# The ramp of a spectral-filter and SiLU kernel on Trainium2: first stage by parts of the position index, eight PSUM banks, second products issued two groups ahead, weight roundings moved

## The chip, the core and the metric

The kernel runs on one core of one Trainium2 chip. The metric is the device time of one execution in microseconds (us); the time of a version is the median of several runs. Engines are named as the profile names them: PE (TensorE, with PEld for its weight loads), DVE (VectorE), ACT (ScalarE), POOL (GpSimd) and SP (SyncE, which here only issues DMAs). ACT and POOL issue DMAs too.

## The reference, cut to what matters

```python
# x [8, 3008, 256]; filt_r, filt_i [1505, 256]
X = np.fft.rfft(x, axis=1)
Y = X * (filt_r + 1j * filt_i)[None]
y = np.fft.irfft(Y, n=3008, axis=1)          # [8, 3008, 256]
# bridge: 24064 tokens of 256 channels; w_in [256, 2048], w_out [2048, 256]
h = y.reshape(24064, 256) @ w_in
g = h * (1.0 / (1.0 + np.exp(-h)))
out = g @ w_out
```

The MLP's weights arrive as 64-bit floats. The kernel reads them as words and rounds them to 32 bits itself.

## The kernel before, in words

**Main stage.** Each batch's 3008 tokens are cut in six pairs of token blocks (`PAIRS` by two halves), 48 pairs in all, and each pair takes 8 steps, one for each 256 columns of the hidden layer: 384 steps. In a step `hidden` computes the products with w_in into the PSUM tiles px (tag "x") and pyz (tag "yz"), with sums and SiLU on DVE and ACT, and `project` multiplies the step before with w_out into four accumulators (tags a0 to a3). Each step also carries pieces of the next batch's transform, put at written-out places by `plan`.

**Ramp.** Before step 0 the transform of batch 0 has to be done at least for half of its tokens, and the first weights have to be rounded. This part is written out in its own order, lines 865 to 931, and the schedule is manual: every engine executes its instructions in the order in which the code issues them, and waits at each for what that one needs. The pieces are:

- `load_first` (L275) loads batch 0 into two tiles: positions n' 0 to 23 of each row into the space of w_t, positions 24 to 31 into x_all.
- `stage1_first(k)` (L289), k = 0 to 15, 16 channels each: two matmuls (L293) into one PSUM bank, 384 columns from the first tile and 128 columns from the second, and a 32x32 block transpose on DVE (L295) into t2.
- `forward(g)`, g = 0 to 5: 32 matmuls (L428) into two banks pb. It needs all 16 transposes.
- `multiply(g, k)`: two DVE products (L443) of a bank with the two filter tables, into the tiles z (four buffers) and p (two buffers in each of two pools). With two k this makes four products a group, each 128x512.
- `add(g, k)`: two POOL instructions (L451, L452) that combine z and p. For the groups in `by_tensor` there is no add, and PE does the sum with twice the matmuls.
- `inverse_first(g, added)`: 32 matmuls (L485), or 64 for the groups in `by_tensor`, into two banks pc; then two ACT copies into q (L490), each stored by an ACT-issued DMA (L492) into the DRAM array d2. A group makes 8 of the 48 rows of d2. The 64-matmul form reads the tables `neg`, which lie in the two buffers of tag "t".
- `load_t4(g, first, last)`: loads rows of d2 in another layout, in two DMAs (h = 0, 1; L517). Groups 2 and 3 use the buffers of tag "t" in the ramp, so these loads wait until PE is done with `neg`.
- `stage3(g)`, g = 0 to 3: 64 PE records (L529) into two banks pd, each copied to y by `evac`, which alternates between DVE (L244) and ACT (L246).
- `weights(j)` loads the words of weight block j (two DMAs of 256 KB, L781 and L784, on SP). `rounded(j...)` rounds a pair of blocks (L801 to L818, DVE and ACT by turns), places them in w_t (L827), and, after the odd block, makes four combinations (L611) in `combine_weights`.
- `bank` (L251) hands out PSUM banks for batch 0 by turns from six: two of tag "f" and a0 to a3.

22 dummy matmuls (tile "idle", tag "x") run on PE at the start. In the order before, the groups follow each other: forward, multiply, add (not in groups 1, 4, 5), the roundings of blocks 2 and 3 behind group 1's products and of blocks 4 and 5 behind group 4's, and `inverse_first(g - 1)` one group later. The first rows of t4 (0 to 39) are loaded ahead of `rounded(6, 7)` and the last inverse, rows 40 to 47 behind it, half of those on POOL's queue. Then `rounded(8)`, and stage 3. The first matmul px of step 0 needs all eight y copies.

DMAs issued from SP and ACT report on eight semaphores by turns. A DMA waits for the last one on its own semaphore to land before it is issued, and the engine that issues it waits with it.

Of the kernel before, what the change touches and what calls it, by code (L numbers as in the profile page):

```python
# [46 lines left out]
FP32 = mybir.dt.float32  # L47
# [6 lines left out]
B, S, C = 8, 3008, 256  # L54
DFF = 2048
N1, N2 = 47, 64
NS, NG = 24, 6
# [110 lines left out]
def kernel(  # L168
# [9 lines left out]
    nc = tc.nc  # L178
# [10 lines left out]
    def pool(name, bufs, space=None):  # L189
        kw = {} if space is None else {"space": space}  # L190
        return ctx.enter_context(tc.tile_pool(name=name, bufs=bufs, **kw))
# [17 lines left out]
    xps = pool("xps", 1, PSUM)  # L209
# [3 lines left out]
    wx_t = cpool.tile([96, 128], FP32)  # L213
# [9 lines left out]
    x_all = xpool.tile([128, 2, 2, 2 * C], FP32)  # L223
# [14 lines left out]
    flip, early = [0], [0]  # L238

    def evac(dst, src):  # L240

        flip[0] ^= 1
        if flip[0]:
            nc.vector.tensor_copy(out=dst, in_=src)  # L244
        else:
            nc.scalar.copy(out=dst, in_=src)  # L246
# [3 lines left out]
    def bank(b, name, spare=None):  # L250


        if b > 0 and spare is not None:
            return accps.tile([128, 2, C], FP32, name=name, tag=f"a{spare}")
        if b > 0 or early[0] is None:
            return fps.tile([128, 2, C], FP32, name=name, tag="f")
        early[0] += 1
        k = early[0] % 6
        if k < 2:
            return fps.tile([128, 2, C], FP32, name=name, tag="f")  # L260
        return accps.tile([128, 2, C], FP32, name=name, tag=f"a{k - 2}")

    def spectral(b):
# [4 lines left out]
        xs, us, t2s, banks, prods, halves, t4s = {}, {}, {}, {}, {}, {}, {}  # L268
# [17 lines left out]
            us["t2"] = view[:, 6144:14336].rearrange("p (s c) -> p s c", c=C)  # L286
            return view

        def stage1_first(k):  # L289

            ps = bank(b, f"pa_{b}_{k}").rearrange("p a c -> p (a c)").rearrange("p (n c) -> p n c", c=16)
            for i, n0, n in ((0, 0, 24), (1, 24, 8)):
                nc.tensor.matmul(out=ps[:, n0:n0 + n], lhsT=wx_t, rhs=xs[i][0:96, :, 16 * k:16 * k + 16],  # L293
                                 start=True, stop=True)
            nc.vector.transpose(out=us["t2"][:, :, 16 * k:16 * k + 16].rearrange("p s c -> p c s"),  # L295
                                in_=ps.rearrange("p n c -> p c n"))

        def load_x(u):

# [20 lines left out]
        def stage1(u):  # L320
            t1 = tpool.tile([128, 2, 2, C], FP32, name=f"t1_{b}_{u}", tag="t")
            ps = [bank(b, f"pa_{b}_{u}_{h}") for h in range(2)]
            if b == 1:
                xt = xs.pop(u)
# [185 lines left out]
        def load_t4(g, first=0, last=2 * NS):  # L510
            if first == 0 and b == 0 and g in (2, 3):
                t4s[g] = tpool.tile([128, 4, C], FP32, name=f"t4_{b}_{g}", tag="t")
            elif first == 0:
                t4s[g] = t4pool.tile([128, 4, C], FP32, name=f"t4_{b}_{g}", tag="t4")
            for h in range(2):
                queue = nc.gpsimd if first > 0 and h == 1 else nc.sync
                queue.dma_start(out=t4s[g][64 * h + first:64 * h + last],  # L517
                                in_=d2[first:last, 4 * g:4 * g + 4, h, :])

        def stage3(g):  # L520
            half, n0 = divmod(4 * g, 16)
            ps = [bank(b, f"pd_{b}_{g}_{h}").rearrange("p a c -> p (a c)")[:, 0:8 * N1]
                  .rearrange("p (a i n) -> p a i n", a=2, i=4) for h in range(2)]
            for cb in range(2):
                for i in range(4):
                    for c0 in (0, 64):
                        for h in range(2):
                            rows = slice(64 * h, 64 * h + 2 * NS)
                            nc.tensor.matmul(  # L529
                                out=ps[h][c0:c0 + 64, cb, i, :],  # L530
                                lhsT=t4s[g][rows, i, 128 * cb + c0:128 * cb + c0 + 64],
                                rhs=wi_t[rows, :], start=True, stop=True)
            if g < 6 and (b > 0 or g > 3):
                load_t4(g + 2)
            if n0 == 0:
                y[b, half] = ypool.tile([128, 2, HALF], FP32, name=f"y_{b}_{half}", tag="y")
            dst = y[b, half].rearrange("p a (r h n) -> p a h n r", h=2, n=16)
            for h in range(2):
                evac(dst[:, :, h, n0:n0 + 4], ps[h])

        return dict(load_first=load_first, stage1_first=stage1_first, load_x=load_x, sums=sums, stage1=stage1, reverse_x=reverse_x,
                    load_fold=load_fold, fold=fold, stage1_fold=stage1_fold, evict_fold=evict_fold,
# [64 lines left out]
    v, gp = nc.vector, nc.gpsimd  # L607
    ty, g_t, acc, unfinished = {}, {}, {}, []

    def combine(eng, out, in0, in1, op):  # L610
        eng.tensor_tensor(out=out, in0=in0, in1=in1, op=op)  # L611
# [149 lines left out]
    def load_weights(j):  # L761

        if j in (8, 13):
            raw = upool.tile([128, 2, 512], U32, name=f"raw_{j}", tag="u")
        else:

            if j in (0, 2):
                raws["at"] = ypool.tile([128, 2, HALF], FP32, name=f"raw_{j}", tag="y").rearrange(
                    "p a n -> p (a n)").bitcast(U32)[:, 0:2048]
                raws["y"] = raws["at"]  # L770
            elif j in (4, 11):
                raws["at"] = raws["s"] = spool.tile([128, 2048], U32, name=f"raw_{j}", tag="s")
# [12 lines left out]
        raws[j] = raw  # L785
# [55 lines left out]
    def combine_weights(jp, part=None):  # L841

        def w(c):
            return w_t[:, jp, c]
        if part != 1:
            combine(v, w(S1), w(S3), w(A22), ALU.add)
            combine(v, w(S2), w(S1), w(A11), ALU.subtract)
        if part != 0:
            combine(v, w(S3), w(A11), w(S3), ALU.subtract)
            combine(v, w(S4), w(A12), w(S2), ALU.subtract)  # L850

    def weights(*js):
        for j in js:
            if wide:
                load_weights(j)

    def rounded(*js, part=None):

        if wide and part != 1:
            round_weights(*js)  # L860
        for j in js:
            if wide and part != 0:
                place_weights(j)
            if not wide and part != 0:
                load_exact(j)
# [7 lines left out]
        for i in range(2):  # L873
            nc.gpsimd.memset(bias_t[32 * j:32 * j + 32, 3 + i:4 + i], 1.0 if j % 2 == i else -1.0)

    ps = xps.tile([128, 512], FP32, name="idle", tag="x")
    for _ in range(22):
        nc.tensor.matmul(out=ps[:, 0:128], lhsT=wx_t, rhs=wx_t, start=True, stop=True)
    part, second = spectral(0), spectral(1)
    weights(0, 1)  # L880
    place = part["load_first"]()
# [16 lines left out]
    for i, scale in enumerate((-1.0, bias_t[:, 4:5])):  # L898
        t = tpool.tile([128, 4, C], FP32, name=f"neg_{i}", tag="t").rearrange("p a c -> p (a c)")
        neg.append(t[:, 0:128 * NG].rearrange("p (g k n) -> p g k n", g=NG, k=2))  # L900
        nc.scalar.activation(out=neg[i], in_=e_t[:, :, :, 0], func=AFT.Identity, scale=scale)
    for k in range(16):
        part["stage1_first"](k)
    for u in range(2):
        second["load_x"](u)
    rounded(0, 1, part=1)
    by_tensor = (1, 4, 5)
    for g in range(NG):
        part["forward"](g)
        for k in range(2):  # L910
            part["multiply"](g, k)
        if g == 0:
            combine_weights(0)
        if g not in by_tensor:
            for k in range(2):
                part["add"](g, k)
        if g in (1, 4):
            rounded(*((2, 3) if g == 1 else (4, 5)))
            weights(*((9, 10) if g == 1 else (11, 12)))
        if g > 0:  # L920
            part["inverse_first"](g - 1, g - 1 not in by_tensor)
    for g in range(4):
        part["load_t4"](g, 0, 40)
    rounded(6, 7)
    part["inverse_first"](NG - 1, False)
    for g in range(4):
        part["load_t4"](g, 40, 2 * NS)
    rounded(8)
    weights(13)
    for g in range(4):  # L930
        part["stage3"](g)
    early[0] = None
# [79 lines left out]
```

## Time and profile before

| What | Value |
|---|---|
| median of 9 runs | 2616.73 us (2615.58 to 2618.15) |
| the profiled execution, its own time | 2617.84 us |
| its span | 2616.0 us |
| mean granted PE clock | 0.989 |
| PE busy over the span | 2570.1 us (98%) |
| DVE, ACT, POOL busy | 65%, 42%, 16% |
| first matmul px of step 0 starts at | 100.92 us |
| PE busy in the first two slices of 40 | 0.7 and 0.7 (in tenths 7, 7), 0.9 or more from the third on |

Busy time counts the instructions that the profiler recorded on an engine. A PE matmul with 32-bit data leaves two records. "Granted clock" is the TensorE clock as a share of full speed; the profile gives it for any stretch of the span. A view by stages gives, for each stretch, the length, then busy us (and instructions) of PE, PEld, DVE, ACT and POOL, then the granted clock, the share of the DMA engines and their GB/s. In the chain of waits, each line has a start, a length and a piece of work, and each piece was released by the one before it.

### The profile page before, as it was taken

The page shows a single profiled execution, that of the slowest core. Times are in us where ns is not written, and L with a number is a line of the kernel's source. Part 1 is how long each engine was busy: PE and PEld are TensorE (multiplying, and loading weights), DVE is VectorE, ACT ScalarE, POOL GpSimd, SP SyncE. Part 2 cuts the span into 40 slices and gives each one's busy share as a digit, 9 for nine tenths or more (in the row PEclk, how much of TensorE's full clock was granted, in tenths as well). Part 3 has the DMA queues.
Part 4 walks back from the last instruction along what each step waited for, and adds up shares of the span by engine and source line. Part 5 has one row for each costly group of instructions (what it writes and reads, how often), then busy time and mean ns, then how long its engine had stood idle before and what let it go on. Part 6 is the DMA issues. An engine that isn't in the chain of part 4 may idle for free.

```text
span 2616.0 us, 48142 instructions
## 1 busy us (share of the span) xinstructions
PE 2570.1 (98%) x18828; PEld 2184.7 (84%) x18828; DVE 1703.6 (65%) x3588; ACT 1106.9 (42%) x3013; POOL 420.2 (16%) x660
## 2 busy tenths in 40 slices
PE   7799999999999999999999999999999999999998
PEld 4578888888888888888888888888888888888987
DVE  6666766676666666667666676666766666555555
ACT  2443444444444444444444444444444444444443
POOL 1121121112111211121113111211122112101100
PEclk8799999999999999999999999999999999999999
DMA  8431222212322122222222222232223311211000
GB/s 263 126 97 53 62 70 72 70 46 64 82 68 65 51 81 64 57 66 75 68 52 66 73 70 60 68 77 54 66 65 71 78 45 29 57 21 21 9 16 16
DMA packets 200236, 171.06 MB, mean 65 GB/s; under 512 B 122276, under 2 KB 174212, under 8 KB 199220
## 3 DMA queue, kind: packets, MB, share of 16 engines
q1 hardware_dynamic: 178664, 117.20, 18.4%
q0 software_dynamic: 16832, 44.20, 5.4%
q10 hardware_dynamic: 4512, 6.59, 0.8%
q8 instruction: 148, 2.42, 0.4%
q14 instruction: 80, 0.66, 0.1%
HBM read 96.05 MB, written 81.26 MB: 68 GB/s over the span
## 4 chain that ended last, share of the span: by engine, by line
PE 94%; DVE 2%; DMA 2%; ACT 1%; issue 0%; ACTq 0%; SPq 0%; POOL 0%; DVEq 0%; POOLq 0%
PE acc L699 43%; PE px L640 25%; PE pyz L640 19%; PE pd L529 3%; PE pb L428 2%; PE pc L464 2%; PE pf L398 1%; DVE g L611 1%; PE pa L335 0%; DMA w_t<-in_x_dram 0%; PE pc L485 0%; DVE w_t L611 0%; DMA filt<-in_filt_r_dram 0%; DMA d_t<-d_tbl 0%; DMA raw<-in_moe_w_in_dram 0%
## 5 line engine op out<-in xcount | busy, mean ns | idle before, releaser
L699 PE MATMUL acc<-g,w_t 128*128 128x256 f32 (+1 forms) x5376 | 1512.1, 375 | 0.4 <-DVE g L611 0.4
L699 PEld LDWEIGHTS acc<-g,w_t 128*128 128x128 f32 x5376 | 1021.3, 190 | 115.7 <-DVE g L611 0.8
L611 DVE TENSOR_TENSOR g<-pyz,abc 128x256 f32<-128x256 f32 (+1 forms) x1152 | 480.3, 417 | 537.6 <-ACT abc L661 297.3
L611 DVE TENSOR_TENSOR g<-g 128x256 f32<-128x256 f32 (+3 forms) x1152 | 617.3, 536 | 197.3 <-ACT g L644 184.1
L640 PE MATMUL px<-ty,w_t 128*128 128x256 f32 (+1 forms) x2304 | 686.8, 380 | 0.5 <-ACT abc L661 0.5
L644 ACT ACTIVATE g<-g 128x256 f32<-128x256 f32 (+1 forms) x1152 | 474.1, 412 | 245.3 <-DVE g L611 245.3
L611 POOL TENSOR_TENSOR s<-s 128x256 f32<-128x256 f32 (+1 forms) x329 | 260.0, 807 | 1454.1 <-DVE s L717 1437.8
L640 PEld LDWEIGHTS px<-ty,w_t 128*128 128x128 f32 x2304 | 424.0, 190 | 83.0 <-issue 25.1
L640 PE MATMUL pyz<-y,w_t 128*128 128x256 f32 (+1 forms) x1536 | 453.6, 377 | 0.7 <-DVE g L611 0.6
L640 PEld LDWEIGHTS pyz<-y,w_t 128*128 128x128 f32 x1536 | 283.4, 189 | 46.5 <-DVE g L611 5.9
L655 ACT COPY abc<-px 128x256 f32<-128x256 f32 (+1 forms) x384 | 141.7, 369 | 364.1 <-PE px L640 364.1
L644 ACT ACTIVATE g<-px 128x256 f32<-128x256 f32 (+1 forms) x384 | 146.4, 381 | 307.2 <-PE px L640 307.2
L661 ACT COPY abc<-px 128x256 f32<-128x256 f32 (+1 forms) x384 | 144.1, 375 | 309.4 <-PE px L640 309.4
L640 PE MATMUL px<-y,w_t 128*128 128x256 f32 (+1 forms) x768 | 229.8, 381 | 1.0 <-ACT y L246 1.0
L640 PE MATMUL pyz<-ty,w_t 128*128 128x256 f32 (+1 forms) x768 | 225.6, 375 | 0.0
L640 PEld LDWEIGHTS px<-y,w_t 128*128 128x128 f32 x768 | 142.1, 189 | 40.0 <-ACT g L644 15.5
L640 PEld LDWEIGHTS pyz<-ty,w_t 128*128 128x128 f32 x768 | 146.0, 190 | 16.9 <-DVE g L611 0.5
L648 ACT COPY abc<-px 128x256 f32<-128x256 f32 (+1 forms) x384 | 135.3, 352 | 2.7 <-PE px L640 1.3
L244 DVE COPY y<-pd 128x376 f32<-128x376 f32 x64 | 51.6, 806 | 107.2 <-PE pd L529 107.2
L529 PEld LDWEIGHTS pd<-wi_t,t 48*64 48x64 f32 x4096 | 68.8, 140 | 31.6 <-issue 31.5
L246 ACT COPY y<-pd 128x376 f32<-128x376 f32 x64 | 51.8, 809 | 99.0 <-PE pd L529 99.0
L529 PE MATMUL pd<-wi_t,t 48*64 48x47 f32 x4096 | 76.6, 239 | 11.6 <-DMA t<-d 9.9
(94 smaller groups left out, 1329.7 us busy)
## 6 DMA issues: line engine op xcount, KB each, us to landing
t<-d SPq DMA_DIRECT2D x120, 192.0 KB
t<-d SPq DMA_DIRECT2D x84, 256.0 KB
d<-q POOLq DMA_DIRECT2D x84, 256.0 KB, 2.6
out_dram<-o SPq DMA_DIRECT2D x636, 32.0 KB
d<-tf POOLq DMA_DIRECT2D x144, 96.0 KB, 2.4
xr<-in_x_dram SPq DMA_DIRECT2D x6, 1472.0 KB
x_all<-in_x_dram SPq DMA_DIRECT2D x72, 96.0 KB
x_all<-xr SPq DMA_DIRECT2D x72, 96.0 KB
```

What stands on the lines that cost most here:

```text
L244: nc.vector.tensor_copy(out=dst, in_=src)
L246: nc.scalar.copy(out=dst, in_=src)
L428: nc.tensor.matmul(out=ps[k][32 * j:32 * j + 32, ri, :], lhsT=d_t[rows, 4 * g + at, ri, :], rhs=t2[rows, at, :], start=True, stop=True)
L464: nc.tensor.matmul(out=ps[j][64 * k:64 * k + 64, a, :], lhsT=e_t[rows, g + a, k, ri, :], rhs=zs[k][rows, ri, :], start=(a == 0 and ri == 0 ...
L529: nc.tensor.matmul(out=ps[h][c0:c0 + 64, cb, i, :], lhsT=t4s[g][rows, i, 128 * cb + c0:128 * cb + c0 + 64], rhs=wi_t[rows, :], start=True, ...
L611: eng.tensor_tensor(out=out, in0=in0, in1=in1, op=op)
L640: nc.tensor.matmul(out=out, lhsT=w_t[:, jp, c, 0], rhs=rhs, start=start, stop=True, skip_group_check=True)
L644: nc.scalar.activation(out=g[:, k, 0:n], in_=g[:, k, 0:n] if src is None else src, func=AFT.Silu)
L648: nc.scalar.copy(out=sums[:, 0, 0:n], in_=xo)
L655: nc.scalar.copy(out=sums[:, 1, 0:n], in_=xo)
L661: nc.scalar.copy(out=sums[:, 2, 0:n], in_=xo)
L699: nc.tensor.matmul(out=acc[pair][i][:, h, 0:n], lhsT=w_t[:, jp, c, 1], rhs=g[:, k, 0:n], start=(jp == 0 and h == 0), stop=last, skip_group ...
```

## The change

Only the ramp is changed.

1. The first dummy matmuls become 36 (22 before), in a bank from `bank`. 34 more stand ahead of stage 3.
2. `bank` hands out eight banks: tags "x" and "yz" join the six.
3. `stage1_first(k, i)` issues one of its two matmuls. The 384-column parts (i = 0) run four k ahead of the 128-column parts, which are followed by the transposes.
4. `forward` runs two groups ahead: forward(0) and forward(1) stand before the loop, forward(g + 2) inside it, and `inverse_first(g)` follows in the same turn for g below 4. `by_tensor` is (2, 4, 5), (1, 4, 5) before; group 1's sum goes to POOL and group 2's to PE.
5. `rounded(2, 3)` moves behind group 2's products, with `combine_weights(0)` behind it (behind group 0's products before). `rounded(4, 5)`, `rounded(6, 7)` and `rounded(8)` stand behind all products. The last two inverses follow `rounded(4, 5)`.
6. `load_x` of batch 1 and `weights(9, 10)` are issued behind group 3; a one-row POOL memset of x_all behind group 3's adds is what the x loads wait for. `weights(11, 12)` are issued behind the last t4 loads.
7. t4's rows are loaded as 0 to 31 (behind group 3) and 32 to 47 (behind `rounded(6, 7)`); the half of the second part that POOL issued is issued by ACT.
8. The four y copies of stage 3's groups 0 and 1 are all on ACT.

```diff
-        k = early[0] % 6
+        k = early[0] % 8
         if k < 2:
             return fps.tile([128, 2, C], FP32, name=name, tag="f")
+        if k > 5:
+            return xps.tile([128, 2, C], FP32, name=name, tag="x" if k == 6 else "yz")
         return accps.tile([128, 2, C], FP32, name=name, tag=f"a{k - 2}")
...
-        def stage1_first(k):
+        def stage1_first(k, i):
+            if i == 0:
+                banks[k] = bank(b, f"pa_{b}_{k}").rearrange("p a c -> p (a c)").rearrange(
+                    "p (n c) -> p n c", c=16)
+            n0, n = ((0, 24), (24, 8))[i]
+            nc.tensor.matmul(out=banks[k][:, n0:n0 + n], lhsT=wx_t, rhs=xs[i][0:96, :, 16 * k:16 * k + 16],
+                             start=True, stop=True)
+            if i == 1:
+                nc.vector.transpose(...)
...
-                queue = nc.gpsimd if first > 0 and h == 1 else nc.sync
+                queue = nc.scalar if first > 0 and h == 1 else nc.sync
...
             for h in range(2):
-                evac(dst[:, :, h, n0:n0 + 4], ps[h])
+                if early[0] is not None and g < 2:
+                    nc.scalar.copy(out=dst[:, :, h, n0:n0 + 4], in_=ps[h])
+                else:
+                    evac(dst[:, :, h, n0:n0 + 4], ps[h])
...
-    for _ in range(22):
-        nc.tensor.matmul(out=ps[:, 0:128], lhsT=wx_t, rhs=wx_t, start=True, stop=True)
+    idle(36)
...
     for k in range(16):
-        part["stage1_first"](k)
-    for u in range(2):
-        second["load_x"](u)
+        part["stage1_first"](k, 1)
+        if k < 12:
+            part["stage1_first"](k + 4, 0)
     rounded(0, 1, part=1)
-    by_tensor = (1, 4, 5)
+    by_tensor = (2, 4, 5)
+    for g in range(2):
+        part["forward"](g)
     for g in range(NG):
-        part["forward"](g)
         for k in range(2):
             part["multiply"](g, k)
-        if g == 0:
-            combine_weights(0)
         if g not in by_tensor:
             for k in range(2):
                 part["add"](g, k)
-        if g in (1, 4):
-            rounded(*((2, 3) if g == 1 else (4, 5)))
-            weights(*((9, 10) if g == 1 else (11, 12)))
-        if g > 0:
-            part["inverse_first"](g - 1, g - 1 not in by_tensor)
+        if g + 2 < NG:
+            part["forward"](g + 2)
+        if g == 2:
+            rounded(2, 3)
+            combine_weights(0)
+        if g < 4:
+            part["inverse_first"](g, g not in by_tensor)
+        if g == 3:
+            gp.memset(x_all[0:1, :, 0, 0:1], 0.0)
+            for u in range(2):
+                second["load_x"](u)
+            weights(9, 10)
+            for later in range(4):
+                part["load_t4"](later, 0, 32)
+    rounded(4, 5)
+    for g in (4, 5):
+        part["inverse_first"](g, False)
+    rounded(6, 7)
     for g in range(4):
-        part["load_t4"](g, 0, 40)
-    rounded(6, 7)
-    part["inverse_first"](NG - 1, False)
-    for g in range(4):
-        part["load_t4"](g, 40, 2 * NS)
+        part["load_t4"](g, 32, 2 * NS)
+    weights(11, 12)
     rounded(8)
     weights(13)
+    idle(34)
     for g in range(4):
         part["stage3"](g)
```

(The four leading calls `stage1_first(k, 0)`, k = 0 to 3, stand ahead of that loop.)

More of the change, by code (lines that the diff above doesn't have):

```diff
@@ L287, in load_first @@
             return view
-        def stage1_first(k):
[L291 to L296, printed above, removed]
+        def stage1_first(k, i):
[6 more added lines that the diff above has]
+            if i == 1:
+                nc.vector.transpose(out=us["t2"][:, :, 16 * k:16 * k + 16].rearrange("p s c -> p c s"),
+                                    in_=banks.pop(k).rearrange("p n c -> p c n"))
         def load_x(u):
@@ L874, with idle @@
             nc.gpsimd.memset(bias_t[32 * j:32 * j + 32, 3 + i:4 + i], 1.0 if j % 2 == i else -1.0)
-    ps = xps.tile([128, 512], FP32, name="idle", tag="x")
-    for _ in range(22):
-        nc.tensor.matmul(out=ps[:, 0:128], lhsT=wx_t, rhs=wx_t, start=True, stop=True)
+    def idle(n):
+        ps = bank(0, "idle").rearrange("p a c -> p (a c)")
+        for _ in range(n):
+            nc.tensor.matmul(out=ps[:, 0:128], lhsT=wx_t, rhs=wx_t, start=True, stop=True)
+    idle(36)
     part, second = spectral(0), spectral(1)
@@ L901 @@
         nc.scalar.activation(out=neg[i], in_=e_t[:, :, :, 0], func=AFT.Identity, scale=scale)
+    for k in range(4):
+        part["stage1_first"](k, 0)
     for k in range(16):
-        part["stage1_first"](k)
-    for u in range(2):
-        second["load_x"](u)
+        part["stage1_first"](k, 1)
+        if k < 12:
+            part["stage1_first"](k + 4, 0)
     rounded(0, 1, part=1)
-    by_tensor = (1, 4, 5)
+    by_tensor = (2, 4, 5)
+    for g in range(2):
+        part["forward"](g)
     for g in range(NG):
-        part["forward"](g)
         for k in range(2):
             part["multiply"](g, k)
-        if g == 0:
-            combine_weights(0)
         if g not in by_tensor:
```

## The prediction, made before the changed kernel ran

> **What bounds it now.** I read the engine line of the page first (PE 98%): from the third of 40 slices on PE is full, and nothing there is touched. The change can only move the ramp, which ends with the first px at 100.92. So I read that stretch alone, first by stages of 5 us:
>
> ```profile
> 15.00:20.00 5.00, 2.86 (x6) 1.44 (x7) 0.41 (x1) 0.19 (x1) 0.00 (x0) 0.50 0.58 197
> 40.00:45.00 5.00, 4.05 (x40) 1.67 (x46) 4.97 (x9) 0.00 (x0) 2.00 (x3) 0.66 1.04 327
> 65.00:70.00 5.00, 3.81 (x72) 2.35 (x64) 4.22 (x9) 4.26 (x8) 0.00 (x0) 1.00 0.01 3
> 85.00:90.00 5.00, 0.00 (x0) 0.00 (x0) 2.48 (x5) 0.28 (x1) 1.23 (x2) 0.59 0.36 126
> 95.00:100.00 5.00, 4.95 (x178) 4.67 (x171) 2.09 (x4) 2.09 (x3) 0.00 (x0) 0.50 0.01 3
> ```
>
> After the length come PE, PEld, DVE, ACT and POOL. The reader is to see DVE (third pair) near full in the two middle rows, no engine full in the fourth, and a granted clock of 0.50 in the first stage and in stage 3. The chain of waits says who ends last:
>
> ```profile
> 45.38 0.73 ACT scratch L803
> ...
> 54.58 0.72 POOL z L451
> ...
> 56.73 3.79 PE pc L485 x30
> 60.51 1.91 PE pb L428 x32
> ...
> 74.93 5.73 PE pc L485 x62
> 80.68 0.60 ACT q L490
> 81.30 0.33 ACTq L492
> 81.67 0.59 ACT q L490
> 82.28 5.79 DMA d<-q
> ...
> 88.15 2.31 DMA t<-d
> 90.54 0.41 PE pd L529 x2
> 92.67 7.34 PE pd L529 x254
> 100.03 0.80 ACT y L246
> 100.92 0.77 PE px L640
> ```
>
> Roundings, products, POOL adds and inverses take turns, none hidden by another; then come 20 us (80.7 to 100.9) of copy, store, load, stage 3 and copy in a row, in which DVE has only 7.2 us of rounding (80.64 to 87.86). The view of waits adds PE pd behind DMA t, 9.9 us. The change puts DVE work beside that tail.
>
> **First stage.** Dummies: 22 (44 records) ran from 3.81 to 12.33, in the stages of 1 us 6 to 7 records until 11, then 11. So 28 more, at 10 to 11 a us, end at 14.9 to 15.3; the x tile lands at 15.1. Before, PE stood from 12.33 to 15.22 and the clock was 0.50 from 15 to 24.5: the first transposes started at 19.59, 21.30, 23.00, 24.69 (1.71 us apart), the rest follow at 0.87. With a full clock and four 384-column parts done ahead (0.65 us each, 15.2 to 17.9, before the second tile lands at 18.70), the first transpose starts at about 19.2 and DVE sets the pace: 19.2 + 15 x 0.87 + 1.04 = 33.3 instead of 36.2, **2.9 us** sooner. If the clock is low all the same, some 1.7 of it is lost. The gap of 17.9 to 18.7 is shorter than the 1.9 us after which the clock fell behind the dummies (at 14.3, from 0.63 as the mean of 14 to 15).
>
> **Groups 0 to 2.** L827 takes 1.39 with 0.16 overlapped: DVE is at the products at 34.5. Four products are 4 x 0.60 = 2.41, so groups 0 and 1 end at 39.4 (filters: the last was waited for by a weight load that left at 38.9; raw 2 and 3 need to be there by 44, as before). Group 2's z reuses group 0's buffer, so DVE now **waits for inverse 0** on PE. POOL starts 0.15 behind the second product (35.95) and its four adds at 0.69 end at 38.75; what is left of the inverse took 2.8 us at the low clock (42.07 to 44.88), about 1.4 at full. DVE waits until 40.2 to 41.5; group 2 ends at 42.6 to 43.9. Queued behind that wait are the roundings, and PE and ACT wait for those.
>
> `rounded(2, 3)` needs ACT, and ACT now has **four copies and four stores ahead of it**. Inverse 1 ends at about 43 (POOL's next four adds end at 41.5), the copies are 0.59 each, and each store waits for an older load on its semaphore; the third waits for a load of weight block 6 that, in the trace, held another issue until 45.59. So ACT begins at about 47.2 (bounds 43.6, nothing in the way, and 49, an inverse at the low clock) against 45.38. From ACT's start to the end of the combinations were 7.74 us (45.38 to 53.12); `combine_weights(0)` adds 1.5 (four L611, 71.52 to 73.07; the 2.79 at 39.83 had POOL beside it). **T = 47.2 + 7.7 + 1.5 = 56.4** (53 to 58.5). Before, DVE was at 53.12 with one group fewer, one inverse fewer.
>
> **From T on.** Group 3's products end at T + 2.4, POOL's adds at T + 4.05. PE has stood since about 50, so the clock is low: forward 5 takes 1.91 to T + 4.3, inverse 3 takes 3.79 to T + 8.1. Group 4's products lie beside that; group 5's wait for inverse 3 (buffer z again) and end at T + 10.5. Then DVE has all roundings without a gap: 8.2 us a pair (64.80 to 73.0; 75.39 to 83.6) and 4.28 for block 8 (83.58 to 87.86): T + 18.7, T + 26.9, **T + 31.2**. Beside it PE, busy since T + 2.4 (before, the clock rose 3.8 to 5.7 us after such a start, at 45.0, 62.0 and 79.1), does inverses 4 and 5 at 3.7 each (45.88 to 49.56), to T + 15.5. ACT is free of the roundings of 4 and 5 at T + 14.5, then copies and stores at 1.0 us each: the last store leaves at T + 18.3, just ahead of ACT's part of `rounded(6, 7)` (T + 19 to T + 22.7). Then ACT issues t4's rows. They need the last store landed: 2.6 us (median of the POOL-issued stores) to 5.79, so T + 20.9 to T + 24.1. Landing takes 2.31 more, stage 3 starts at T + 25 to T + 26.5. POOL's four issues before took 2.39, with 4.6 to landing, and PE stood 1.7 us on them: off the path now. [...]
>
> The second dummies (68 records) end at about T + 22.5, 2 to 4 us ahead of stage 3; in the trace the clock fell 1.9 to 5.3 us after PE stopped (14.3 after 12.3, 55.2 after 51.7, 85.9 after 80.65). I take half a chance. Stage 3 is 7.34 at the low clock, 4 x 0.95 at full (64 records in 1.15 later in the span, 0.2 of it the last one's tail). ACT's copies begin after its part of block 8, T + 28.7, and six at 0.82 make **T + 33.6**; with a low clock the last pd comes at T + 33.2 and ends as T + 34.1. I take px at T + 34 = 90.4: **10.5 us** sooner. Step 0 lasted 7.1 us from px to the last L661, with 6.5 us of PE work at half clock; at full clock ACT and DVE would bound it at about 5.5, so 0 to 1.6, I take 0.5. Later loads stay covered: x and blocks 9, 10 leave at T + 4 and are needed at T + 34, blocks 11, 12 leave at T + 26 and are needed two steps of 8 us later than that. If a load came late, step 0 would wait for the rest of its landing, 5 us at most by the rows. Eight banks cost nothing that a row shows; without them the four parts ahead would not fit.
>
> **Sum**: 2617.84 - 10.5 - 0.5 = 2606.8 for the profiled execution; it was 1.1 above the median, so **2606** as a median. About 0.2% (5.2 us, 2611.5) is what a measurement of this kernel can tell from no change.
>
> **The rivals.**
> - *Shorter, 2600.* T at 53 to 54 (ACT not in the way), inverse 3 at full clock (T + 5.5 instead of T + 8.1), step 0 at full clock: 3 + 2.6 + 1.1 less. For it: DMA traffic in 40 to 55 is lighter, as x and blocks 9, 10 are gone from there. Against: DMA share 1.04 there, the low clocks above.
> - *A chain of DMA waits, 2611.* Group 5's stores wait on semaphores last used by the first t4 loads, and these wait for group 3's stores. With 5.8 for each store and 4.9 for each load, ACT's part of `rounded(6, 7)` comes at T + 22.8, and t4's last rows behind stores landed at T + 28.2: px at T + 38.8, 95.2.
> - *Slower, 2618.* The clock stays at 0.50 from inverse 2 to step 0. For it: PE was busy 4.95 of 5 us in stage 3 and stayed at 0.50 from 92.7 to 106.7. Place: inverses 4 and 5 at 6.85 each (73.8 to 80.65) end at T + 21.8, the dummies, at 5.2 records a us (44 in 8.52), hold PE until T + 34.9, stage 3 until T + 42.2, px at T + 43.2. That passes 100.9 from T = 57.7; at T = 58.5 it is 101.7, 0.8 later. Against: three rises of the clock while inverses ran. [...]
> - *The dummies do not hold the clock*: 1.7 less gain, 2607.5, inside the range.
>
> **Chances.** Forecast (2603 to 2609) 0.60, shorter 0.17, DMA chain 0.14, slower 0.06, something in the main stage 0.03. The range runs from the shorter case to just past the DMA chain, 2600 to 2612, and takes in T from 53 to 58.5 and both landings. Faster by over 0.2%: 0.60 + 0.17 + half of the DMA chain, and a little of the rest, 0.85. Slower by over 0.2% needs the low clock and a late T together, 0.04; within 0.2% the rest, 0.11.
>
> **What will show it.** Transposes at one pace from 19.2 on, ending at 33.3; a wait of DVE z for PE pc of 1 to 2 us at 39 and of 3 us at T + 5; ACT's rounding start near 47; roundings without a gap from T + 10.5; px near 90, with steps of 8 us behind it as before. It is wrong if px comes after 96, or if px is early and the later steps lose it again.

## The result, and the profile after

The changed kernel takes 2607.08 us as a median of 9 runs (2605.24 to 2609.09), against 2616.8 for the kernel before in the same session: ratio 0.9963, 95% interval 0.9955 to 0.9971, so 9.7 us or 0.37% faster. The profiled execution has a time of its own of 2608.44 us and a span of 2606.7 at a clock of 0.992. The first px starts at 91.66, 9.26 us sooner. One execution among the experiments below, the profiled one of e4, ran at a granted clock of 0.556 from end to end and took 4498.77 us; no time and no reading below goes by it.

The ramp by stages, the changed kernel (length; busy us of PE, PEld, DVE, ACT, POOL; clock; DMA share; GB/s):

```profile
15.00:20.00 5.00, 5.00 (x22) 3.24 (x21) 1.97 (x3) 0.00 (x0) 0.00 (x0) 1.00 0.68 212
40.00:45.00 5.00, 5.00 (x119) 2.81 (x120) 3.83 (x8) 1.77 (x3) 1.37 (x2) 1.00 0.90 284
50.00:55.00 5.00, 0.00 (x0) 0.00 (x0) 4.86 (x12) 2.05 (x4) 0.00 (x0) 0.63 0.31 115
65.00:70.00 5.00, 5.00 (x100) 3.33 (x96) 4.34 (x9) 3.22 (x7) 0.00 (x0) 1.00 0.97 316
85.00:90.00 5.00, 5.00 (x191) 4.86 (x188) 3.96 (x10) 4.24 (x7) 0.00 (x0) 0.50 0.63 190
95.00:100.00 5.00, 4.47 (x14) 2.40 (x13) 3.37 (x8) 3.57 (x9) 1.73 (x4) 0.94 0.25 70
```

The first stage now has the full clock (first row, 0.50 before). DVE is no longer full in 40 to 45 (3.83, 4.97 before), PE does nothing from 50 to 55, and from 65 to 70 PE is full with inverses 4 and 5 (3.81 before) beside DVE's rounding. Stage 3 (85 to 90) runs at 0.50 in spite of the dummies ahead of it; from 95 to 100 the clock is 0.94, 0.50 before, and the kernel is in step 0. ACT's timeline shows where T comes from (start, length, engine and line; in brackets how long it stood and for what):

```profile
41.81 0.34 ACTq L497 DMA_DIRECT2D d<-q  x1
43.13 0.59 ACT L495 COPY q<-pc 128x512 f32<-128x512 f32 x1 [1.35 <-PE pc L490]
44.91 0.33 ACTq L497 DMA_DIRECT2D d<-q  x1
45.28 0.59 ACT L495 COPY q<-pc 128x512 f32<-128x512 f32 x1 [1.56 <-DMA raw<-in_moe_w_in_dram]
46.91 0.33 ACTq L497 DMA_DIRECT2D d<-q  x1
47.28 0.72 ACT L811 ACTIVATE scratch<-scratch,bias_t 128x512 f32<-128x512 uint32 x1 [1.41 <-DMA d<-q]
```

The copies themselves take 0.59. The two stores of group 1 held ACT for 1.56 and 1.41 us, once for a weight load and once for an older store, and only then could the rounding of blocks 2 and 3 begin. DVE pays for it, and then waits for inverse 3:

```profile
48.55 0.69 DVE L821 SCALAR_TENSOR_TENSOR scratch<-raw,scratch 128x512 f32<-128x512 uint32 x1 [4.42 <-ACT scratch L813]
...
56.48 0.69 DVE L448 TENSOR_TENSOR z<-pb,filt 128x512 f32<-128x512 f32 x1
...
64.82 0.69 DVE L448 TENSOR_TENSOR z<-pb,filt 128x512 f32<-128x512 f32 x1 [3.47 <-issue]
```

T is 56.48. The chain of waits from there (start, length, work):

```profile
59.11 1.96 PE pb L433 x30
61.06 3.67 PE pc L490 x32
64.74 0.58 ACT q L495
...
66.32 5.48 DMA d<-q
...
72.74 4.38 DMA t<-d
...
77.19 3.30 DMA d<-q
...
80.56 2.21 DMA t<-d
...
83.01 7.74 PE pd L534 x256
...
90.77 0.79 ACT y L246
...
91.66 1.19 PE px L648 x2
```

Two PE pieces (1.96 and 3.67 us) at a clock of 0.50, which lasts from 51.25 to 64.90, then store, load, store, load (15.4 us of flight), then stage 3 at 0.50: the roundings on DVE, forecast as the row that sets the end, are not in the chain at all. They end close to it all the same. DVE's last rounding, before and after:

```profile
87.10 0.76 DVE L827 TENSOR_TENSOR w_t<-scratch 128x256 f32<-128x256 f32 x2
```

```profile
88.83 0.76 DVE L835 TENSOR_TENSOR w_t<-scratch 128x256 f32<-128x256 f32 x2
```

It ended at 87.86, 13.06 us ahead of px, and now ends at 89.59, 2.07 ahead: the long tail without work on DVE is what the change took away. The roundings are late themselves. The two stores of group 5 stood for t4's first loads, and ACT and DVE stood with them (ACT, then DVE):

```profile
75.85 0.59 ACT L495 COPY q<-pc 128x512 f32<-128x512 f32 x1 [1.98 <-DMA t<-d]
77.57 0.72 ACT L811 ACTIVATE scratch<-scratch,bias_t 128x512 f32<-128x512 uint32 x1 [1.13 <-DMA t<-d]
```

```profile
78.84 0.69 DVE L821 SCALAR_TENSOR_TENSOR scratch<-raw,scratch 128x512 f32<-128x512 uint32 x1 [2.00 <-ACT scratch L813]
```

DVE's last copy of y then waited 0.40 for stage 3, at 90.73.

Behind step 0 nothing is given back in the steps. The 31st copy abc<-px (step 10) starts 10.02 us sooner than before, the last one of the kernel 10.00, and so do the last transposes. First a line of the chain of before, then the same one of after:

```profile
2609.64 0.65 DVE o L729 x2
```

```profile
2599.64 0.65 DVE o L737 x2
```

The spans differ by 9.3 only (2616.0 and 2606.7): behind these lines stand the last output stores alone, which took some 0.7 longer there, and the change touches nothing of them.

### The profile page after: what moved, and what is told of

It reads as the page before. It is cut to its first block, busy times and chain, and to the rows that moved or that the text cites. A ratio compares the mean times of both kernels' runs of the same rounds, so it can differ in the third digit from the quotient of the medians.

```text
span 2606.7 us, 48336 instructions
## 1 busy us (share of the span) xinstructions
PE 2572.4 (99%) x18924; PEld 2191.5 (84%) x18924; DVE 1700.0 (65%) x3586; ACT 1107.8 (42%) x3015; POOL 417.7 (16%) x657
## 4 chain that ended last, share of the span: by engine, by line
PE 96%; DMA 1%; DVE 0%; ACT 0%; issue 0%; SPq 0%; DVEq 0%; ACTq 0%
PE acc L707 43%; PE px L648 26%; PE pyz L648 19%; PE pd L534 3%; PE pb L433 2%; PE pc L469 2%; PE pf L403 1%; PE pa L340 0%; PE pa L331 0%; DMA t<-d 0%; DMA d<-q 0%; PE pc L490 0%; DVE g L619 0%; DVE w_t L619 0%; DVE s L619 0%
```

## The experiments

The changed kernel and all experiments but e4 (told further below) in one table. T is the start of group 3's products, px the first px in the chain of waits, "gain" how much sooner step 10 starts than in the kernel before; the steps keep a gain to within 0.1 us up to the last one. These columns come from one execution each, the ratios from several. The code ahead of T is the same in the changed kernel, e7, e10 and e11, and T varies from 56.24 to 58.22 among them, so px - T tells more of what lies behind T. But the code behind T is the same in the changed kernel, e2 and e6, and px - T varies from 34.77 to 36.26 among those. A difference smaller than these, 2.0 us in T and 1.5 in px - T, is not shown by one execution.

| run | T | px | px - T | gain | ratio to before (95%) |
|---|---|---|---|---|---|
| changed kernel | 56.48 | 91.66 | 35.18 | 10.02 | 0.9963 (0.9955 to 0.9971) |
| e1, first stage alone | | 97.38 | | 3.78 | 0.9991 (0.9982 to 1.0) |
| e2, all but the first stage | 58.58 | 94.84 | 36.26 | 6.42 | 0.9975 (0.9965 to 0.9985) |
| e6, 22 first dummies | 58.22 | 92.99 | 34.77 | 8.14 | 0.9976 (0.9967 to 0.9985) |
| e3, loads early | 56.30 | 90.72 | 34.42 | 10.89 | 0.9961 (0.9948 to 0.9975) |
| e7, t4's rows on POOL | 57.39 | 95.48 | 38.09 | 6.06 | 0.9977 (0.9968 to 0.9986) |
| e8, stores from SP | 54.26 | 90.80 | 36.54 | 10.95 | 0.9962 (0.995 to 0.9975) |
| e9, e3 and e8 | 54.38 | 88.08 | 33.70 | 13.30 | 0.9945 (0.9932 to 0.9959) |
| e10, 46 second dummies | 58.22 | 92.91 | 34.69 | 8.14 | 0.9967 (0.9956 to 0.9978) |
| e11, no second dummies | 56.24 | 91.90 | 35.66 | 8.66 | 0.9967 (0.9955 to 0.998) |
| e12, e9 and PE kept busy | 52.66 | 88.54 | 35.88 | 13.38 | 0.9952 (0.994 to 0.9965) |
| e13, the same mended, late blocks | 54.40 | 84.88 | 30.48 | 15.88 | 0.9941 (0.9927 to 0.9954) |

**The two halves of the change.** e1 is the kernel before with `idle(36)`, `stage1_first(k, i)` and eight banks; e2 is the changed kernel with the old first stage:

```diff
-    idle(36)
+    idle(22)
...
-    for k in range(4):
-        part["stage1_first"](k, 0)
     for k in range(16):
-        part["stage1_first"](k, 1)
-        if k < 12:
-            part["stage1_first"](k + 4, 0)
+        part["stage1_first"](k)
```

(The definition of `stage1_first` goes back with it.)

> The kernel before with only the new first stage (36 dummies, parts by n' with four ahead, eight banks); order of groups, roundings and t4 as before. My theory: the transposes end near 32.3 as in the changed kernel, and since DVE is near full from 36 to 53 in the kernel before, the 3.9 us come through to the first px: 97.0 to 97.9 instead of 100.92, time 2613 to 2614. Rival, loads: blocks 2 and 3 or a store's older load hold ACT's rounding of (2,3), which began at 45.38: then that start moves by 1 us or less, px at 100 or later, 2616. If the split alone were the source of the whole gain of the change, the time would be near 2607.

> The changed kernel with the first stage of before (22 dummies, both parts of a bank together, in order); eight banks, the new order, the second dummies and t4's rows are kept. My theory: transposes end near 36.2, but ACT's rounding of (2,3) was held in the changed kernel by a store that waited for a load until 44.91, so T (DVE at the products of group 3) moves from 56.48 by less than the 3.9 us: by 1.5 to 2.5. px at 93 to 94.2, time 2608.5 to 2609.7. Rival, the pace comes through: px at 95.6, 2611. Rival, loads alone set T: px at 91.7, 2607.

e1's trace came as the first theory said: transposes end at 32.97, ACT's rounding starts at 42.18 instead of 45.38, px at 97.38. Its median, 2615.12, is 2.4 us under before, where 2613 to 2614 were expected; the trace's gain is 3.78. e2 lies between theory and first rival. T moved by 2.1 us, as expected, but T varies by as much with the same code, so this does not decide between the two; px - T grew by 1.1 behind the same code. Its median, 2611.29, is 6.2 under before. The halves add up in the traces, 3.78 + 6.42 = 10.20 against 10.02, and nearly in the medians, 2.4 + 6.2 = 8.6 against 9.7. So the first stage brings 2.4 to 3.8 us and the reorder some 6.3. No run takes the reorder apart: what the eight banks, PE's sum of group 2 in place of group 1, t4's cut at row 32 and the y copies on ACT are worth alone stays open.

e6 is the changed kernel with `idle(22)`:

> The changed kernel with 22 dummies instead of 36 ahead of the first stage. It tells the dummies from the split. My theory: with PE standing from 12.3 to 15.1 the clock is 0.50 to about 24; four first parts take 1.3 each, the first transpose starts at 20.5 to 21, the next two 1.7 apart, then 0.87: transposes end at 35 to 36.5, so the split without the dummies is worth 1 us at most. px then as in the run with the order alone, 93 to 94. Rival, the four parts ahead give the pace whatever the clock: transposes end by 33.5, px within 0.5 of 91.66.

The expectation for the transposes was wrong. The first came late, at 20.14, but all 16 followed at one pace and ended at 34.45, against 36.19 before, 35.80 in e2 and 32.28 to 33.97 in the runs with 36 dummies. So, by one trace of each, the parts ahead are worth 1.4 to 1.7 without the dummies, and the 14 dummies 0.5 to 2.2 on top. px, at 92.99, was expected, but it can't be laid to the dummies alone, as T was 58.22 in e10 too, with 36 of them.

**The chain of DMA waits.** e3 sends batch 1's x and blocks 9 and 10 sooner:

```diff
             rounded(2, 3)
+            v.memset(x_all[0:1, :, 0, 0:1], 0.0)
+            for u in range(2):
+                second["load_x"](u)
+            weights(9, 10)
             combine_weights(0)
...
-            gp.memset(x_all[0:1, :, 0, 0:1], 0.0)
-            for u in range(2):
-                second["load_x"](u)
-            weights(9, 10)
```

> The changed kernel with the second batch's x and blocks 9 and 10 sent behind the rounding of blocks 2 and 3 (near 52 to 54, when the queues are empty from 55 to 60) instead of just ahead of group 3's stores. My theory (chain of store, load, store, load): group 3's second store lands in 2.5 to 3.5 us instead of 5.48, t4's first rows leave near 69.5, ACT's stores of groups 4 and 5 no longer wait for them, and stage 3 starts near 81 instead of 83.01: px at 89.5 to 90.2, time 2605.5 to 2606. Rival, DVE's and ACT's roundings set the end: px at 91.2 or later, 2607. Rival, the early loads collide with group 2's stores: T moves later, px past 92.

t4's first rows leave at 68.21, 2.1 us behind group 3's second store (66.13); it was 5.6 in the changed kernel. Group 5's last store leaves at 74.78 instead of 77.19 and stage 3 starts at 80.47 instead of 83.01. px gains only 0.9 of these 2.5, because stage 3 waits 1.25 us within its first group for a row, runs at 0.50 and ends at 89.8. So the loads were the cause of the long landing, and a stage 3 at 0.50 stood behind it. The ratio, 0.9961 against 0.9963, can't tell e3 from the changed kernel; 2605.5 to 2606 were expected, the median was 2607.45.

e8 issues the stores of the ramp's inverses from SP:

```diff
-                nc.scalar.dma_start(out=d2[a0:a0 + 4].rearrange("a n h c -> (a n) h c"), in_=qt)
+                nc.sync.dma_start(out=d2[a0:a0 + 4].rearrange("a n h c -> (a n) h c"), in_=qt)
```

e9 is e3 and e8 together.

> The changed kernel with the inverses' stores (two each) issued by SP instead of ACT, so that a store that waits for an older transfer holds no copy and no rounding. My theory: ACT's rounding of (2,3) starts at 43.9 to 44.6 instead of 47.28, DVE's wait of 4.42 falls to 1.5, T is 53.3 to 54 instead of 56.48; ACT's waits ahead of the rounding of (6,7) (1.98 and 1.13) go, and the loads of x, 9 and 10 leave behind group 3's stores instead of ahead. px at 86.5 to 89, time 2602 to 2605. Rival, T is set by DVE or by the loads of blocks 2 and 3: T at 56 or later and px at 91 to 92, 2607. Rival, SP's own order makes the stores late (it issues x, 9, 10 and t4's first rows between them): T early but px at 91 or later.

> Stores from SP and the loads of x, 9 and 10 sent behind the rounding of (2,3), together. My theory: T at 53.3 to 54 as with the stores alone; the early loads are gone from the stretch of t4's first rows, so px is another 0.5 to 1.5 sooner, 85.5 to 88, time 2601 to 2604. Rival, with T sooner the roundings on DVE set the end (8.2, 8.2 and 4.3 us in a row behind group 5's products, then copies): px no sooner than T + 33.6, 87 to 87.6, the same as with the stores alone. Rival, the loads at T - 3 collide with group 2's stores and the gain of the stores is lost: px at 90 or later.

ACT's timeline in e9, the same place as above:

```profile
44.20 1.08 ACT L495 COPY q<-pc 128x512 f32<-128x512 f32 x2 [1.85 <-PE pc L490]
45.16 0.73 ACT L811 ACTIVATE scratch<-scratch,bias_t 128x512 f32<-128x512 uint32 x1
```

The rounding follows the copies at once, 2.1 us sooner (45.05 in e8), and T is 54.3 in both, 1.9 under the lowest T with the new order and the stores on ACT (56.24): ACT's waits set T. In e8 the second rival came true as well. SP, in its order, issued t4's first rows until 73.49, so group 4's stores left at 74.00 (71.92 in the changed kernel) and px gained only 0.9; the ratio, 0.9962, is the changed kernel's. With the loads out of the way (e9) the stores of groups 4 and 5 leave at 70.73 to 72.60 and px comes at 88.08. What bounds it then shows on DVE in e9:

```profile
62.50 0.69 DVE L448 TENSOR_TENSOR z<-pb,filt 128x512 f32<-128x512 f32 x1 [3.25 <-issue]
...
85.48 0.80 DVE L244 COPY y<-pd 128x376 f32<-128x376 f32 x1
87.14 0.79 DVE L244 COPY y<-pd 128x376 f32<-128x376 f32 x1 [0.87 <-PE pd L534]
```

From group 5's products to the copies of y DVE has no wait over 1.0 us, nearly as the forecast had it; left are 3.25 ahead of the row (inverse 3, which took 3.5 us there and 2.2 in e13) and 0.87 at its end (stage 3, whose last 87 records took 2.59 us, as long as 145 in e10 at a clock of 1.00).

**t4's rows on POOL.** e7 gives the half of t4's second rows back to POOL:

```diff
-                queue = nc.scalar if first > 0 and h == 1 else nc.sync
+                queue = nc.gpsimd if first > 0 and h == 1 else nc.sync
```

> The changed kernel with t4's second rows issued by POOL again. My theory: as before, four issues of POOL take 2.4 us and land in some 4.6 instead of 2.2, so the last group of stage 3 waits: PE through with stage 3 at 91.5 to 93, px 1 to 2.3 us later (92.7 to 94), time 2608 to 2609.5. Rival, the roundings on DVE set the end (89.6): px within 0.4 of 91.66. [...]

PE in e7:

```profile
83.93 0.42 PE L534 MATMUL pd<-wi_t,t 48*64 48x47 f32 x2 [3.54 <-DMA t<-d]
85.35 4.73 PE L534 MATMUL pd<-wi_t,t 48*64 48x47 f32 x167 [1.00 <-issue]
91.92 2.59 PE L534 MATMUL pd<-wi_t,t 48*64 48x47 f32 x87 [1.83 <-issue]
```

px - T is 2.9 us longer, in two waits within stage 3. Stage 3 itself starts at T + 26.5 in both kernels, and the four issues lay at T + 24.6 to T + 26.3 with POOL and T + 24.3 to T + 26.3 with ACT, so nothing was lost in issuing. The first wait is for POOL's row of group 0, issued at 82.02 and used at 85.35, 3.3 us; ACT's, issued at 80.75, was used at 83.01, 2.3 us. But ACT's row took 2.7 in e9, 3.2 in e3 and 3.5 in e12, where PE waits at the same place for 0.68 to 1.72 us. The second wait is told under the hardware below and comes with other edits too. So the ratios put this kernel 3.7 us above the changed one (their intervals just touch, at 0.9968 to 0.9971), while no more than 1.1 us of it can be pointed at in the trace as POOL's, and one execution can't settle even that. The size is open between 0 and 2.9 us.

**The second dummies.** e4 and e10 are the same edit, e11 takes the row away:

```diff
-    idle(34)
+    idle(46)
```

> The changed kernel with 46 instead of 34 dummies ahead of stage 3: at 0.116 us a record they end at 82.3 instead of 79.4, 0.7 ahead of stage 3 (83.0), so that the clock should be full there. [...] My theory: stage 3 takes 3.8 to 5 us instead of 7.7, but ACT comes free of block 8 only at 86.9 and DVE at 89.6, and six copies on ACT at 0.72 to 0.8 end at 91.2 to 91.4: first px 0.2 to 0.5 us sooner (91.2 to 91.5), time 2607. Rival, stage 3 sets the end: px at 88 to 89, 2604. Rival, the clock is low in stage 3 all the same: px at 91.7 and stage 3 at 7.7.

> The same edit as in the run with 46 dummies, whose profiled execution was throttled as a whole (clock 0.556, 4497 us), so that its trace says nothing on stage 3. Theories as there: with ACT and DVE as the bound, stage 3 at full clock and first px at 91.2 to 91.7; with stage 3 as the bound, px at 88 to 89; with a low clock all the same, px at 91.7 or later. The other six executions of that run had a median near 2610.4, 3 above the changed kernel's: if that is real, the longer row of dummies holds stage 3 back in executions where t4's rows land early, and the trace should show PE still in the dummies when the last of the first rows of t4 have landed, or the clock falling for step 0.

> The changed kernel without the 34 dummies ahead of stage 3. Stage 3 ran at 0.50 there in spite of them, so my theory is no change: px within 0.7 of 91.66, time 2606.5 to 2608. Rival, the dummies hold the clock for other executions or shorten its way back up in step 0: px 0.5 to 2 us later or step 0 longer than 6.2 us, 2608 to 2609.5.

PE in e10:

```profile
72.17 10.54 PE L888 MATMUL idle<-wx_t 96*128 96x128 f32 x92
83.64 2.59 PE L534 MATMUL pd<-wi_t,t 48*64 48x47 f32 x145 [0.94 <-DMA t<-d]
88.70 3.24 PE L534 MATMUL pd<-wi_t,t 48*64 48x47 f32 x111 [2.46 <-issue]
92.91 1.19 PE L648 MATMUL px<-y,w_t 128*128 128x256 f32 x2 [0.97 <-ACT y L246]
```

The dummies did hold the clock (1.00 from 82 to 88), and 145 records ran in 2.59 us (7.74 for 256 at 0.50 in the changed kernel). Then PE stood 2.46 us and did the rest at 0.50, and the last copies of y on DVE waited 0.59 and 0.91 for it. px - T is 34.69, 0.5 less than in the changed kernel, as the first theory had it; but e6, with the 34 dummies, has 34.77, so this is not to be laid to the 12 more. Both runs of the edit have a ratio slightly above the changed kernel's (0.9972 with 0.9961 to 0.9983, and 0.9967), and the intervals overlap: no difference that can be measured; T was 1.7 later in e10's profiled execution. Without dummies (e11) px came at 91.90, as the theory had it. From T to step 10 this run takes 1.6 us more than the changed kernel: px - T is 0.5 longer, and step 0 takes 7.36 instead of 6.21 us from px to its last abc copy. But e2, which has the 34 dummies, takes 1.5 more as well (114.34 against 112.84, e11 114.44), and the ratios, 0.9967 and 0.9963, overlap. So no run shows that the second dummies are worth anything.

**Keeping PE busy.** e12 puts 26 dummies behind inverse 2 into that inverse's own bank, on top of e9. e13 puts them into inverse 1's bank, sends blocks 11 and 12 behind `rounded(8)`, and has 44 dummies ahead of stage 3:

```diff
+            if g == 1:
+                us["pc"] = ps[0].rearrange("p a c -> p (a c)")
+            if g == 2:
+                for _ in range(26):
+                    nc.tensor.matmul(out=us["pc"][:, 0:128], lhsT=wx_t, rhs=wx_t, start=True, stop=True)
...
+            if j == 11:
+                v.memset(raw[0:1, :, 0:1].bitcast(FP32), 0.0)
...
-    weights(11, 12)
     rounded(8)
+    weights(11, 12)
     weights(13)
-    idle(34)
+    idle(44)
```

> Stores from SP and early loads as in the run with both, and 26 dummies on PE between inverse 2 and forward 5, in inverse 2's bank behind its first copy. PE stood there from 48.7 to 55.8 and the clock was 0.50 from 51.8 to 62.0, so forward 5 took 1.95 and inverse 3 3.5 us, and DVE's group 5 waited 3.25 for it. My theory: with a full clock these take 1.0 and 2.0, POOL's adds are ready at T + 4.05, group 5 starts at 59.9 to 60.5 instead of 62.5, and since DVE's roundings run without a gap from there to the copies of y, px is 2 to 2.6 us sooner: 85.5 to 86.2, time 2600 to 2601.5. Rival, the clock falls all the same (PE stands 1 to 1.6 us ahead of the dummies): px within 0.4 of 88.05. Rival, stores and t4's rows take over as the bound: group 5 sooner by 2, px by less than 1.

> Stores from SP and early loads as in the run with both, and three edits on what was seen there: 26 dummies behind inverse 2 in inverse 1's bank (empty since about 45), so that PE does not stand from 48.7 on; blocks 11 and 12 sent behind the rounding of block 8 (by a memset of one element of their buffer on DVE) instead of just behind t4's second rows; 44 dummies ahead of stage 3. My theory: forward 5 and inverse 3 at full clock take 1.0 and 2.0, DVE's group 5 starts at T + 5.7 to 6.2 instead of T + 8.1; t4's last row lands in 2 to 3 us; stage 3 runs at full clock and is hidden behind block 8's rounding, and the row on DVE and ACT from group 5 to the last copy of y (24.7 us without a wait) alone sets the end: px at 84.5 to 86, time 2599.5 to 2601.5. Rival, t4's rows and a stage 3 at low clock set the end: group 5 early, but px at 87 to 88.5, as in the run with both, 2603 to 2605. Rival, the dummies hold forward 5 back as in the run before: group 5 at T + 8 or later and px past 88.

e12's dummies did not help: its ratio and its gain are no better than e9's, and group 5 starts at T + 8.85 where e9 has T + 8.12. Their bank had to be copied by ACT first, and the copy waited for group 0's store to land (44.11 + 5.94):

```profile
50.77 7.70 PE L499 MATMUL pc<-wx_t 96*128 96x128 f32 x52 [3.68 <-ACT q L495]
58.40 1.09 PE L433 MATMUL pb<-w_t,d_t 64*32 64x256 f32 x32
```

So PE stood 3.68 us, the dummies took 7.70 us where e13's, which do not stand, take 6.07, and forward 5, which could have started at about 54, came at 58.40. The first rival named the place, PE standing ahead of the dummies, but at 1 to 1.6 us. In e13 they begin at once, and the clock is 1.00 in every 5 us from 50 to 80:

```profile
48.76 6.07 PE L497 MATMUL pc<-wx_t 96*128 96x128 f32 x52
...
57.02 1.09 PE L433 MATMUL pb<-w_t,d_t 64*32 64x256 f32 x30 [0.61 <-DVE p L448]
...
77.07 3.85 PE L539 MATMUL pd<-wi_t,t 48*64 48x47 f32 x224
82.16 0.68 PE L539 MATMUL pd<-wi_t,t 48*64 48x47 f32 x32 [1.25 <-issue]
84.88 1.19 PE L653 MATMUL px<-y,w_t 128*128 128x256 f32 x2 [2.04 <-ACT y L246]
```

and the view of waits of DVE from 30 to 86 has nothing long left:

```profile
DVE scratch L828 <- ACT scratch L820: 4.1, 7, 1.2
DVE z L448 <- issue: 1.1, 1, 1.1
DVE z L448 <- POOL z L457: 1.1, 1, 1.1
DVE z L448 <- PE pb L433: 0.9, 1, 0.9
```

Group 5 starts at T + 5.93, stage 3 is through 2 us ahead of px, and the row on DVE and ACT alone sets the end. 2602.15 us as a median (ratio 0.9941, upper end 0.9954, just under the lower end of the changed kernel's), 5.9 us of gain on top of the change by the traces. It has the lowest median of these kernels; against e9 (2602.92) the medians can't tell, the traces have 2.6 us.

## Why the prediction was right, and the steps in which it was not

The forecast was 2606 as a median and px at 90.4; it was 2607.1 and 91.66. Step by step:

- **First stage: right.** 33.3 was forecast for its end, it was 32.28, and in the nine other runs that have it 32.49 to 33.97. Alone it is worth 3.8 us by e1's trace and 2.4 by its median, 2.9 were forecast. One small loss was not seen: PE, through with its parts at 29.1, stood 3.25 us for the last transposes, and the three forwards took 5.4 us at a clock of 0.50, which lasted from 30.77 to 37.60. It cost nothing, since DVE started at 34.38 (34.5 forecast).
- **T: right, with luck in the size, and its cause is shown.** 56.4 forecast, 56.48 measured; ACT's start at 47.2 forecast, 47.28 measured. That both fit to 0.1 is luck, as T goes up to 58.22 with the same code. The lower bound for that start, 43.6 with nothing in the way, was 45.05 to 45.16 when SP issued the stores. The wait was for the block load, as the forecast had taken from the trace of before, and then for an older store, which it had not named. DVE stood 1.05 us ahead of group 2 (1 to 2 forecast), by the profile for POOL's adds, where the forecast had inverse 0.
- **From T to group 5: right.** z at T + 8.1 forecast, T + 8.34 measured; the inverse 3, 3.67 us at a clock of 0.50, is the cause, as e13 shows (clock 1.00, T + 5.93). With the same code from T up to there it took 2.54 us in e6 and 2.60 in e10.
- **"The last store leaves at T + 18.3": this step failed.** It left at T + 20.7. The step let ACT copy and store as soon as its rounding was done. In the run these stores waited on semaphores of t4's first loads (1.98 and 1.13 us), these for group 3's store, and that landed in 5.48 us behind 1.8 MB of loads that the change puts there. The rival "a chain of DMA waits" had this mechanism at 4.8 us and 0.14; it was there at a quarter of that price, 1.2 us of px. e3 and e9 show the mechanism: without the loads the store's reader leaves 2.1 us behind it, and without the loads and the stores on ACT px comes at T + 33.70, where the forecast's row of roundings said T + 33.6.
- **"All roundings without a gap": failed for the same reason.** ACT's part of `rounded(6, 7)` began at T + 21.1, forecast T + 19, DVE stood 2.00 us for it, and its last rounding ended at T + 33.1, forecast T + 31.2. So both rows, the transfers with stage 3 and the roundings, ended late and within half a us of each other; a faster stage 3 alone could have brought some 0.4, an estimate from DVE's last wait (0.40).
- **t4's rows, "off the path now": open.** The forecast's sum has no gain for the move from POOL to ACT. What it is worth stays open between 0 and 2.9 us (e7). The four issues lay alike in both traces (2.23 us of POOL in e7, 2.35 of ACT), so what there is to gain here does not come from issuing.
- **The second dummies, "half a chance": they did not keep stage 3's clock.** PE stood 3.46 us ahead of it, the clock fell at 81.97, and stage 3 took 7.74 us at 0.50. The forecast put 1.7 us on that clock. No run shows such a price: e10, with the clock held for 145 of 256 records, has px at T + 34.69, inside what the same code varies by.
- **Step 0: a gain of 0.5 forecast, 0.8 measured** (6.97 before, 6.21; 6.69 in e2 and 6.80 in e6 with the same code). The sum forecast 11.0 up to there, it was 10.0, and 9.3 at the end of the span by the last stores' landing.

The main stage kept the gain to the last step, as assumed. For the profiled execution 2606.8 was forecast and 2608.44 measured: px came 1.2 us late, step 0 gave 0.3 more than forecast, and the last stores took 0.7.

## What to carry to other kernels

An engine that issues a DMA can stand with it until an older transfer has landed (ACT here for 1.56, 1.41, 1.98 and 1.13 us), so count a store's wait as work of that engine, and look up what else is under way on its semaphore. Bulk loads that are needed late belong where the queues are empty, not just ahead of a store that a load waits for (group 3's store landed in 5.48 us behind them; without them, in e3, the load that waits for it left after 2.1). Where two engines take turns and PE stands for several us, harmless work on PE kept its clock (1.00 from 50 to 80 in e13, where the changed kernel had 0.50 from 51.25 to 64.90). It did not help where it had to wait for a late copy itself (e12, 3.68 us).

## What the runs showed of the hardware

**The granted clock in the ramps.** In the kernel before, the granted clock is by turns 1.00 and 0.50 from 10.85 us on, for 3.41, 10.24, 17.07, 3.41, 10.24, 6.83, 10.24, 6.83, 6.83 and 20.48 us. In the changed kernel it is so from 10.29 on, for 20.48, 6.83, 13.65, 13.65, 17.07 and 13.65. Each of these lengths is a multiple of 3.413 us, to 0.01. How long PE had been busy does not by itself tell the next level. In the changed kernel the clock fell at 30.77, after 3.41 us with PE busy for 1.72, and in the kernel before it stayed at 1.00 beyond 82.52, after 3.41 us with PE busy for 1.54. In the changed kernel PE was busy for 7.68 of the 7.74 us from 83.01 on, and the clock stayed at 0.50 until 95.62. In e6, where all but two records of stage 3 ran from 84.39 on, it was 0.50 from 85 to 87, 0.56 as the mean of 87 to 88, and 1.00 from 88 to 89. What tells these cases apart is not shown.

**PE stands at the same places of its program.** Nine waits within stage 3 that the profile puts down to nothing ("issue") lie at two places of PE's program. They last 0.39 to 2.46 us: 0.39 in e9, 0.41 in e8, 0.44 in e3, 0.97 in e12, 1.05 in e2, 1.25 in e13, 1.64 in e6, 1.83 in e7 and 2.46 in e10. Of the 256 PE records of stage 3, 87 were left behind the wait in e3, e7, e8 and e9, 111 in e10, which has 12 dummies (24 records) more ahead of it, and 60 in e2 and e6, which have 14 (28 records) fewer. Counted from the start, that is behind 852 or 853 records, ahead of the 427th matmul of PE's program (two records each), in all seven runs. In e12 and e13, with 52 and 72 more records of dummies than e9, 11 and 32 were left, so the place is 127 or 128 records further. PE in the changed kernel, at 0.50, had its 853rd record at 87.80 and the next one 0.30 later. What PE waits for there is not shown. It matters for what a faster stage 3 can bring: in e10 it cost 2.46 us, where 256 records at 2.59/145 each, 4.6 us, would have won 3.2 on the 7.74 of the changed kernel, an estimate.
